# Delta-rule attention with a feed-forward part: the state step on 64 rows, behind the Gram run

## The chip, the cores and the metric

The kernel runs on one core of a Trainium2 chip. The metric is the device time of one execution in microseconds. A core has TensorE (PE; its weight loads are listed apart as PEld), VectorE (DVE), ScalarE (ACT), GpSimd (POOL) and SyncE (SP), which here only issues DMAs. Each engine works through its own instructions in a fixed order.

## What is computed

For each of 32 pairs of batch and head there is a 48x48 state that is updated token by token, 768 times; its readings are then the input of a feed-forward part.

```python
k_n = k / (np.linalg.norm(k, axis=-1, keepdims=True) + 1e-06)
for t in range(S):                                   # B, H, S, D = 4, 8, 768, 48
    y[:, :, t] = np.einsum('bhd,bhde->bhe', q[:, :, t], state)
    v_old = np.einsum('bhde,bhd->bhe', state, kt)
    state = state + bt[:, :, :, None] * np.einsum('bhd,bhe->bhde', kt, vt - v_old)
...
h = x @ w_in                                         # x: (3072, 384), w_in: (384, 2048)
return (np.maximum(0.01 * h, h) @ w_out).astype(np.float32)
```

## The kernel before

The 768 tokens are cut into 12 blocks of 64. Inside a block the recurrence is replaced by matrix products with the inverse of a triangular 64x64 matrix for each pair; the state is carried from block to block. The 32 pairs are two groups, g = 0 and 1, of 16; a group's data lies on partitions 64 to 127 (g = 0) or 0 to 63 (g = 1) of its tiles (DATA), and the state on the other half (STATE). Four streams are woven together by the loop at the end of the kernel, which runs over the blocks n and, inside a block, over 17 slots s:

- `ffn(n)` (`ff`): the feed-forward part of block n, one of 16 slices f of the hidden width in each slot. The first products go to `ph` (L735; a pair of slices is issued together, 18 matmuls), ScalarE writes `gh` and again `ph` (L745, L749), VectorE the low half `gl` (L750), and the second products add into `po` (L726), two slices later, six matmuls a slice.
- `solve(n + 1)` (`sv`): the steps of the next block, one in each of the slots that `SV` gives. `load` brings the parts of the inverse (`sq`, `rt`) and runs `pz`, `tie` runs `pu`, `kt` runs `pk` (L624) and scales the values (L640), `step_w` runs `pw` (L649), `step_y` runs `py` (L669), whose result is `ys`, and `step_s` runs `pc` (L659), the new state.
- `gram(n + 3)` (`gg`), in slot 12 in the steady blocks: `pg` (L311) holds keys times keys and keys times queries. ScalarE copies the first to `gs` (L315), SyncE stores them as `gd` (L319) and loads them as `L` (L349); VectorE masks the second into `rq` (L328) and copies corners to `gm` (L336).
- `inv(n + 2)` (`iv`): the elimination on VectorE (L392 `tmp`, L397 `T`), 31 steps of small instructions, begun by `sr` (L368) when `L` has landed. At its end ScalarE copies `T` (L457) and SyncE stores `td` and `tt` (L464, L465), from which `sq` and `rt` are loaded.

The Gram run of block n waits in program order until `solve(n - 2)` is done. `step_s` multiplies 128 rows: 64 of keys (in `rk`) with 64 of corrected values (in `rv`), and below them an identity (written once by `identities`) with the old state, so that TensorE adds the old state itself. The two groups follow each other, 16 matmuls each. ScalarE copies the result to the state rows of the next block's `rv` (L661). Results of TensorE other than `ph` and `po` share four PSUM banks in rotation (`ps_a`), in the order in which the program asks for them. A `with behind(x)` holds an instruction back in the order until the last instruction marked x; where nothing holds it, a scheduler sets the order of each engine.

In the first block VectorE and ScalarE also turn the weights, which come as raw pairs of words, into high and low halves (`conv`, `expand`, `final`, `cast`, `lows`; L193 writes the low halves `w`).

Of the kernel before, what the change touches and what calls it, by code (L numbers as in the profile page):

```python
# [20 lines left out]
D = 48  # L21
# [26 lines left out]
def delta_moe_kernel(ctx: ExitStack, tc, kq0, kqT, kv, qT, beta, cst, w_all, out, nblk):  # L48
# [47 lines left out]
    def of(x, n, g):  # L96
        return ring[x][(n * NGR + g) % NR[x]]
# [6 lines left out]
    def statics():  # L104
        for t in ring["t"]:
            nc.gpsimd.memset(t, 0.0)
        for x in "vq":
            for i, t in enumerate(ring[x]):
                nc.gpsimd.memset(t[SIDE[i % NGR]], 0.0)

    def identities():
        for i, t in enumerate(ring["k"]):
            r = SIDE[i % NGR]
            nc.gpsimd.tensor_copy(
                t[r].rearrange("p h u t -> p (h u) t"),
                eye[r, r.start:r.start + D].rearrange("p (o t) -> p o t", o=1).broadcast_to([R0, GH, D]))


    wi, wo = ([{}, {}] for _ in range(2))
    raws, mark = {}, {}  # L120
# [80 lines left out]
    def need(gen, fn, n):  # L201
        while (fn, n) not in done:
            next(gen)
# [74 lines left out]
    tails, held = [], []  # L278

    def gram(n):  # L280
        need(sv, solve, n - Q_BUFS // NGR)
        kqs = []
        for g in range(NGR):
            t = sb.tile([P, GS, NPAIR, 2, C], F32, tag="kq", name=f"kq{n}_{g}", bufs=KQ_BUFS)
# [272 lines left out]


    LD = 2
    NSLOT = LD + 4  # L560

    def fetch(n, g):
        with behind("kq"):
# [26 lines left out]
    def solve(n):  # L590
# [11 lines left out]

        def tie(g):
            merge_u(n, g, tv(n, g))

        def heads(rows):

            return ((c, u, slice(c * 64, c * 64 + rows)) for u in range(GU) for c in (1, 0))

        def quarters():  # L610

# [40 lines left out]
            mark["rv"] = d.ins  # L652

        def step_s(g):
            k, v, v1 = of("k", n, g), of("v", n, g), of("v", n + 1, g)
            pv = out_of("pc", g, D)
            for c, u, r in heads(D):
                with nullcontext() if n else behind("ph"):
                    nc.tensor.matmul(pv[r, u], k[:, c, u], v[:, c, u], start=True, stop=True)  # L659
            for c in range(2):  # L660
                nc.scalar.copy(v1[STATE[g], c], pv[c * 64:c * 64 + D])  # L661

        def step_y(g):

# [7 lines left out]
            if not n and not g:  # L672
                expand(0, "ys", slice(1, 2))

        stages = [(0, load), (1, tie), (LD, kt), (LD + 1, step_w), (LD + 2, step_y), (LD + 3, step_s)]
        if n in (0, nblk - 1):
            stages.remove((LD + 3, step_s))
        for s in range(NSLOT):
            for g in range(NGR):
                for at, stage in stages:  # L680
                    if at == s:
                        stage(g)
            if s == NSLOT - 1:
                done.add((solve, n))
                if 1 < n < nblk - 1:
                    for g in range(NGR):
                        fetch(n + 1, g)
                if n == 0:
                    columns(0)
                    yield  # L690
                    for g in range(NGR):
                        step_s(g)
            yield
# [93 lines left out]
    def weave_at(i, n, *streams):  # L787

        for gen, steps, a, b in streams:
            key = gen, n, a  # L790
            want = steps if i >= b - 1 else min(steps, max(0, i + 1 - a) * steps // (b - a))
            while taken.get(key, 0) < want:
                next(gen, None)
                taken[key] = taken.get(key, 0) + 1
# [10 lines left out]
    ff = chain(ffn, range(nblk))  # L805
    next(fg)
    statics()
    identities()
    for f in range(KA):
        load_w(f)  # L810
    for g in range(NGR):
# [38 lines left out]
    for n in range(nblk):  # L850

        for s in range(NF):
            at = min(n, 3)
            weave_at(s, n, (ff, NF, 0, NF))
            for fn, *args in work.pop(n * NF + s, ()):
                fn(*args)
            weave_at(s, n, (sv, (NS + (n == 0)) * (n + 1 < nblk), *SV[at]), (iv, NI * (n + 2 < nblk), *IV[at]),
                     (gg, NGR * (n < 2), *GG[min(n, 1)]), (gg, NGR * (0 < n < nblk - 3), *G4[min(n, 2)]))


# [2 lines left out]
KA = 2  # L863
IV, GG = ((9, 17), (6, 17), (2, 17), (2, 17)), ((2, 4), (1, 2))
G4 = (0, 1), (13, 14), (12, 13)
SV = (0, 10), (3, 13), (1, 11), (2, 12)
PD, FB = 2, 4


# [64 lines left out]
```

## Time and profile before

| | |
|---|---|
| time, median of 3 runs | 619.13 us (617.09 to 621.03) |
| profiled execution, its own time | 613.75 us |
| its span, first to last instruction | 612.0 us |
| mean granted clock of TensorE | 0.991 of full speed |
| TensorE busy | 570.2 us, 93% of the span |
| VectorE busy | 431.6 us, 71% |
| ScalarE busy | 329.5 us, 54% |
| GpSimd busy | 40.0 us, 7% |

A profile is of one execution. All windows and timelines count from the start of the span; a busy share is a mean over stretches with different limits, so a row of one stretch says nothing of another.

### The profile page before, as it was taken

The page shows a single profiled execution, that of the slowest core. Times are in us where ns is not written, and L with a number is a line of the kernel's source. Part 1 is how long each engine was busy: PE and PEld are TensorE (multiplying, and loading weights), DVE is VectorE, ACT ScalarE, POOL GpSimd, SP SyncE. Part 2 cuts the span into 40 slices and gives each one's busy share as a digit, 9 for nine tenths or more (in the row PEclk, how much of TensorE's full clock was granted, in tenths as well). Part 3 has the DMA queues.
Part 4 walks back from the last instruction along what each step waited for, and adds up shares of the span by engine and source line. Part 5 has one row for each costly group of instructions (what it writes and reads, how often), then busy time and mean ns, then how long its engine had stood idle before and what let it go on. Part 6 is the DMA issues. An engine that isn't in the chain of part 4 may idle for free.

```text
span 612.0 us, 22386 instructions
## 1 busy us (share of the span) xinstructions
PE 570.2 (93%) x9146; PEld 523.6 (86%) x9146; DVE 431.6 (71%) x1949; ACT 329.5 (54%) x818; POOL 40.0 (7%) x71
## 2 busy tenths in 40 slices
PE   5287989889899989999999999999999999999996
PEld 4266767678799989999999999999999999999996
DVE  3999899969749849759759749759759659331221
ACT  3377976735546446545545545555555545454332
POOL 7000000100040010010010010010010010100100
PEclk9989999999999999999999999999999999999999
DMA  5995933161381461570580580580661550500101
GB/s 128 304 278 207 313 80 74 39 132 31 93 162 33 96 133 33 109 152 14 108 159 7 113 158 5 119 152 12 116 146 29 98 95 4 109 6 4 27 0 27
DMA packets 120103, 59.69 MB, mean 98 GB/s; under 512 B 109248, under 2 KB 110336, under 8 KB 118976
## 3 DMA queue, kind: packets, MB, share of 16 engines
q1 hardware_dynamic: 116896, 52.42, 38.7%
q0 software_dynamic: 2528, 5.12, 3.3%
q8 instruction: 72, 1.18, 0.8%
q10 hardware_dynamic: 576, 0.72, 0.6%
q14 instruction: 31, 0.25, 0.2%
HBM read 46.96 MB, written 11.27 MB: 95 GB/s over the span
## 4 chain that ended last, share of the span: by engine, by line
PE 69%; DVE 18%; DMA 4%; issue 3%; ACT 2%; POOL 1%; SPq 1%; DVEq 0%; ACTq 0%; POOLq 0%
PE ph L735 27%; PE po L726 27%; DVE T L397 4%; DVE tmp L392 4%; PE pw L649 3%; PE py L669 3%; PE pc L659 2%; DVE w L193 2%; PE pg L311 2%; PE pk L624 2%; DVE rq L328 2%; DVE cg L179 1%; DMA L<-gd 1%; DMA sq<-tt 1%; PE pz L494 1%
## 5 line engine op out<-in xcount | busy, mean ns | idle before, releaser
L735 PE MATMUL ph<-xh,w 128*128 128x256 f32 x1056 | 205.6, 285 | 0.0
L726 PE MATMUL po<-w,gh 128*128 128x384 f32 x704 | 178.1, 344 | 0.0
L735 PEld LDWEIGHTS ph<-xh,w 128*128 128x128 f32 x1056 | 168.3, 188 | 4.8 <-issue 3.9
L745 ACT ACTIVATE gh<-ph 128x256 fp32r<-128x256 f32 (+1 forms) x192 | 73.5, 385 | 175.5 <-PE ph L735 112.1
L750 DVE TENSOR_TENSOR gl<-ph,gh 128x256 fp32r<-128x256 f32 x176 | 73.8, 420 | 130.0 <-ACT ph L749 127.4
L735 PE MATMUL ph<-xl,w 128*128 128x256 f32 x528 | 148.3, 283 | 1.6 <-DVE xl L128 1.6
L726 PEld LDWEIGHTS po<-w,gh 128*128 128x128 f32 x704 | 120.6, 188 | 3.7 <-issue 1.8
L726 PE MATMUL po<-w,gl 128*128 128x384 f32 x352 | 111.7, 338 | 2.3 <-DVE gl L750 2.3
L397 DVE TENSOR_TENSOR T<-T,tmp 128x60 f32<-128x60 f32 (+35 forms) x661 | 110.8, 206 | 0.7
L392 DVE TENSOR_TENSOR tmp<-T,L 128x60 f32<-128x60 f32 (+35 forms) x661 | 110.6, 206 | 0.4
L735 PEld LDWEIGHTS ph<-xl,w 128*128 128x128 f32 x528 | 99.5, 188 | 2.5 <-DVE xl L128 2.0
L726 PEld LDWEIGHTS po<-w,gl 128*128 128x128 f32 x352 | 65.3, 188 | 3.1 <-DVE gl L750 3.0
L749 ACT ACTIVATE ph<-ph 128x256 f32<-128x256 f32 x176 | 66.8, 380 | 0.0
L777 POOL DMA_DIRECT2D out<-ob x44 | 23.0, 527 | 482.1 <-ACT ob L776 481.5
L328 DVE TENSOR_TENSOR rq<-pg,csb 64x256 f32<-64x256 f32 x80 | 33.8, 422 | 5.7 <-ACT gs L315 4.1
L735 PE MATMUL ph<-x,cg 128*128 128x256 f32 x96 | 24.5, 407 | 4.3 <-DVE cg L179 2.8
L635 ACT ACTIVATE rt<-pk 48x512 f32<-48x512 f32 x44 | 26.1, 592 | 3.8 <-PE pk L624 3.0
L735 PEld LDWEIGHTS ph<-x,cg 128*128 128x128 f32 x96 | 18.9, 202 | 9.7 <-DVE cg L179 4.4
L661 ACT COPY rv<-pc 48x384 f32<-48x384 f32 x44 | 20.9, 475 | 9.7 <-PE pc L659 9.1
L651 ACT COPY rv<-pw 64x384 f32<-64x384 f32 x48 | 22.8, 475 | 5.5 <-PE pw L649 4.4
L640 DVE TENSOR_TENSOR rv<-rv,nt 64x384 f32<-64x384 f32 x44 | 22.5, 549 | 0.7
L726 PE MATMUL po<-cg,gh 128*128 128x384 f32 x64 | 22.7, 493 | 0.0
(101 smaller groups left out, 587.3 us busy)
## 6 DMA issues: line engine op xcount, KB each, us to landing
wr<-in_w_all SPq DMA_DIRECT2D x8, 1536.0 KB, 12.9
kq<-in_kqT SPq DMA_DIRECT2D x40, 192.0 KB, 4.4
rk<-in_kv SPq DMA_DIRECT2D x24, 192.0 KB, 3.8
rv<-in_kv SPq DMA_DIRECT2D x24, 192.0 KB, 4.0
rq<-in_qT SPq DMA_DIRECT2D x24, 192.0 KB, 3.4
L<-gd SPq DMA_DIRECT2D x18, 256.0 KB, 4.1
out<-ob POOLq DMA_DIRECT2D x44, 96.0 KB, 2.5
td<-T SPq DMA_DIRECT2D x40, 64.0 KB, 2.9
```

What stands on the lines that cost most here:

```text
L328: nc.vector.tensor_tensor(qa[to, c, b * NPAIR:(b + 1) * NPAIR], pv[b][r, 1], tri[r].rearrange("p (o t) -> p o t", o=1).broadcast_to([C, NP ...
L392: nc.vector.tensor_tensor(tv, t[:, :, j:j + 1].broadcast_to([P, k, w]), L[:, j, j + 1:].rearrange("p (o w) -> p o w", o=1).broadcast_to([P ...
L397: mark["steps"] = nc.vector.tensor_tensor(t, t, tv, ALU.subtract).ins
L635: nc.scalar.mul(ts[g][STATE[g], c], pv[g][c * C:c * C + D].rearrange("p (y v) t -> p y v t", y=2), -1.0)
L640: nc.vector.tensor_tensor(v[to, :, us], v[to, :, us], nt[to, g, :, us].rearrange("p h (u o) -> p h u o", o=1).broadcast_to([C, 2, NPAIR, D ...
L651: d = nc.scalar.copy(v[DATA[g], c], pv[c * C:(c + 1) * C])
L726: i = nc.tensor.matmul(po[t][:, :DO], a[:, ts_], w, start=(f == 0 and k == 0), stop=(f == NFC - 1 and k + 1 == len(ways)))
L735: i = nc.tensor.matmul(ph, w[:, cc * P:(cc + 1) * P], a, start=(k == 0), stop=(k + 1 == len(ways)))
L745: i = nc.scalar.activation(gh, ph, AF.Prelu, alpha=0.01)
L749: i = nc.scalar.activation(ph, ph, AF.Prelu, alpha=0.01)
L750: mark["gl"] = nc.vector.tensor_tensor(gl, ph, gh.bitcast(F32), ALU.subtract).ins
L777: nc.gpsimd.dma_start(out[r0:r0 + C], ob[a:a + C])
```

## The change

`step_s` no longer multiplies the identity: it takes the 64 rows of keys and values alone, and `both` gives it the two groups in turn, as `kt` has them, so that four quarters of the array are addressed. VectorE adds the old state while it takes the result out of PSUM; in block 0, where there is none, ScalarE copies as before. The identities go. `step_s` moves one step later, so that in the steady blocks it comes in slot 13, behind the Gram run of slot 12, and with it the end of `solve` and the loads of the next block's keys, values and queries that follow it. The Gram run waits for `step_y` of its block alone. `SV` now lists the slot of each step.

```diff
-    def identities():
-        for i, t in enumerate(ring["k"]):
...
     def gram(n):
-        need(sv, solve, n - Q_BUFS // NGR)
+        need(sv, "y", n - Q_BUFS // NGR)
...
-    NSLOT = LD + 4
+    NSLOT = LD + 5
...
         def step_s(g):
-            k, v, v1 = of("k", n, g), of("v", n, g), of("v", n + 1, g)
-            pv = out_of("pc", g, D)
-            for c, u, r in heads(D):
-                with nullcontext() if n else behind("ph"):
-                    nc.tensor.matmul(pv[r, u], k[:, c, u], v[:, c, u], start=True, stop=True)
-            for c in range(2):
-                nc.scalar.copy(v1[STATE[g], c], pv[c * 64:c * 64 + D])
+            if not g:
+                return
+            vs, v1 = ([of("v", m, g) for g in range(NGR)] for m in (n, n + 1))
+            with nullcontext() if n else behind("ph"):
+                pv = both("pc", D, lambda g, c, u: of("k", n, g)[DATA[g], c, u], lambda g, c, u: vs[g][DATA[g], c, u], D)
+            for g in range(NGR):
+                for c in range(2):
+                    x, to = pv[g][c * C:c * C + D], STATE[g]
+                    if not n:
+                        nc.scalar.copy(v1[g][to, c], x)
+                        continue
+                    with behind("gl"):
+                        nc.vector.tensor_tensor(v1[g][to, c], x, vs[g][to, c], ALU.add)
...
-        stages = [(0, load), (1, tie), (LD, kt), (LD + 1, step_w), (LD + 2, step_y), (LD + 3, step_s)]
+        stages = [(0, load), (1, tie), (LD, kt), (LD + 1, step_w), (LD + 2, step_y), (LD + 4, step_s)]
         if n in (0, nblk - 1):
-            stages.remove((LD + 3, step_s))
-        for s in range(NSLOT):
+            stages.remove((LD + 4, step_s))
+        slots = NSLOT - (not n)
+        for s in range(slots):
...
-            if s == NSLOT - 1:
+            if s == LD + 2:
+                done.add(("y", n))
+            if s == slots - 1:
                 done.add((solve, n))
...
-            want = steps if i >= b - 1 else min(steps, max(0, i + 1 - a) * steps // (b - a))
+            if isinstance(a, tuple):
+                want = sum(t <= i for t in a[:steps])
+            else:
+                want = steps if i >= b - 1 else min(steps, max(0, i + 1 - a) * steps // (b - a))
...
-SV = (0, 10), (3, 13), (1, 11), (2, 12)
+SV = (1, 2, 4, 5, 7, 8, 9, 9), (4, 6, 7, 9, 11, 12, 14), (2, 4, 5, 7, 9, 10, 13), (3, 5, 6, 8, 10, 11, 13)
```

The two lists of each place are of the same steady block, before and after the change; line numbers are those of each kernel. First TensorE, where `pc` stood before: behind the second products of slice 9 and ahead of the first products of slices 12 and 13.

```order
L669 MATMUL py_1_6010<-rv_85,rq_79 32x48 x32
L726 MATMUL po_0_5499<-w_1659,gh_9_5923 128x384 x2
L726 MATMUL po_0_5499<-w_1659,gl_9_5925 128x384
L726 MATMUL po_1_5500<-w_1659,gh_9_5923 128x384 x2
L726 MATMUL po_1_5500<-w_1659,gl_9_5925 128x384
L659 MATMUL pc_0_6068<-rv_84,rk_76 48x48 x16
L659 MATMUL pc_1_6087<-rv_85,rk_77 48x48 x16
L735 MATMUL ph_72<-xh_0_5440,w_1747 128x256
```

And where it stands now, from the end of the Gram run `pg` on.

```order
L303 MATMUL pg_1_1_6170<-kq_1_6128 64x128
L723 MATMUL po_0_5497<-w_1687,gh_11_6055 128x384 x2
L723 MATMUL po_0_5497<-w_1687,gl_11_6057 128x384
L723 MATMUL po_1_5498<-w_1687,gh_11_6055 128x384 x2
L723 MATMUL po_1_5498<-w_1687,gl_11_6057 128x384
L732 MATMUL ph_73<-xh_0_5438,w_1747 128x256
L732 MATMUL ph_73<-xl_0_5439,w_1747 128x256
L732 MATMUL ph_73<-xh_0_5438,w_1747 128x256
L612 MATMUL pc_0_6210<-rv_84,rk_76 48x48 x5
L612 MATMUL pc_1_6211<-rv_85,rk_77 48x48 x5
L612 MATMUL pc_0_6210<-rv_84,rk_76 48x48
L612 MATMUL pc_1_6211<-rv_85,rk_77 48x48
```

The state run went from ahead of the first products of slice 12 to six `po` and three `ph` behind the Gram run, inside the first products of slices 14 and 15, and the groups now take turns.

On VectorE, before, from the last instruction of the elimination to `gl` of slice 15:

```order
L397 TENSOR_TENSOR T_5558<-T_5558,tmp_30_0_6388 128x8
L750 TENSOR_TENSOR gl_12_6150<-ph_72,gh_12_6148 128x256
L750 TENSOR_TENSOR gl_13_6243<-ph_72,gh_13_6241 128x256
L328 TENSOR_TENSOR rq_78<-pg_0_0_6186,csb 64x256 x2
L328 TENSOR_TENSOR rq_78<-pg_0_1_6187,csb 64x256 x2
L328 TENSOR_TENSOR rq_79<-pg_1_0_6215,csb 64x256 x2
L328 TENSOR_TENSOR rq_79<-pg_1_1_6216,csb 64x256 x2
L750 TENSOR_TENSOR gl_14_6288<-ph_73,gh_14_6286 128x256
```

And after the change:

```order
L389 TENSOR_TENSOR T_5556<-T_5556,tmp_30_0_6386 128x8
L747 TENSOR_TENSOR gl_12_6104<-ph_72,gh_12_6102 128x256
L747 TENSOR_TENSOR gl_13_6197<-ph_72,gh_13_6195 128x256
L320 TENSOR_TENSOR rq_78<-pg_0_0_6140,csb 64x256 x2
L320 TENSOR_TENSOR rq_78<-pg_0_1_6141,csb 64x256 x2
L320 TENSOR_TENSOR rq_79<-pg_1_0_6169,csb 64x256 x2
L320 TENSOR_TENSOR rq_79<-pg_1_1_6170,csb 64x256 x2
L655 TENSOR_TENSOR rv_86<-pc_0_6210,rv_84 48x384 x2
L655 TENSOR_TENSOR rv_87<-pc_1_6211,rv_85 48x384 x2
L747 TENSOR_TENSOR gl_14_6286<-ph_73,gh_14_6284 128x256
```

The four adds came in between the eight masks and `gl` of slice 14; nothing else moved here. On ScalarE the four copies of `pc` are gone, and `gh` of slice 12 stands ahead of the copy `T`, where it stood behind it.

On the queue of SyncE, before, from the stores of the elimination's result to the load `L` that the next elimination waits for:

```order
L464 DMA td_6395<-T_5558 32x16x32 x2
L465 DMA tt_6396<-T_5558 1024x1x16
L464 DMA td_6395<-T_5558 32x16x32 x2
L465 DMA tt_6396<-T_5558 1024x1x16
L565 DMA rv_85<-in_kv 64x768
L527 DMA sq_1973<-td_6395 32x8x32
L524 DMA sq_1971<-tt_6396 32x8x32 x3
L319 DMA gd_6178<-gs_0_6184 32x8x32 x4
L319 DMA gd_6178<-gs_1_6214 32x8x32 x4
L524 DMA sq_1971<-tt_6396 32x8x32
L527 DMA sq_1973<-td_6395 32x8x32
L349 DMA L_6177<-gd_6178 64x1024 x2
```

And after the change, to the last of the loads `sq` from `tt`:

```order
L457 DMA tt_6394<-T_5556 1024x1x16
L525 DMA rt_82<-td_6393 32x16x32
L525 DMA rt_83<-td_6393 32x16x32
L311 DMA gd_6132<-gs_0_6138 32x8x32 x4
L516 DMA sq_1969<-tt_6394 32x8x32
L311 DMA gd_6132<-gs_1_6168 32x8x32 x4
L516 DMA sq_1969<-tt_6394 32x8x32
L557 DMA rk_76<-in_kv 64x768
L341 DMA L_6131<-gd_6132 64x1024 x2
L557 DMA rk_77<-in_kv 64x768
L516 DMA sq_1969<-tt_6394 32x8x32 x2
```

Three loads `sq` from `tt` went from ahead of `gd` to behind it, two of them behind `L`; two loads `rt` came ahead of `gd`; and the keys `rk`, which stood ahead of `td`, now surround `L`. The values `rv` are loaded later, outside the piece shown.

## Rows read from the trace of the kernel before

**Rows 1.** Windows, two stretches: start:end, length, busy us and instructions by engine, clock, DMA.

```profile
60.00:122.00 62.00, 57.97 (x819) 43.27 (x817) 58.56 (x185) 48.90 (x78) 2.21 (x4) 0.97 0.47 132
...
325.81:370.65 44.84, 44.84 (x731) 42.22 (x731) 33.15 (x172) 24.06 (x64) 2.08 (x4) 1.00 0.47 94
```

**Rows 2.** Timeline of TensorE, one steady block: start us, us, engine, line, op, tiles.

```profile
325.74 0.62 PE L726 MATMUL po<-w,gh 128*128 128x384 f32 x2
...
326.90 0.28 PE L735 MATMUL ph<-xh,w 128*128 128x256 f32 x1
327.02 0.28 PE L735 MATMUL ph<-xl,w 128*128 128x256 f32 x1
...
330.20 1.58 PE L649 MATMUL pw<-rv,rt 128*32 128x48 f32 x128
...
338.92 1.65 PE L659 MATMUL pc<-rv,rk 128*48 128x48 f32 x64
340.49 0.39 PE L735 MATMUL ph<-xh,w 128*128 128x256 f32 x1
...
344.01 1.94 PE L311 MATMUL pg<-kq 48*64 48x128 f32 x62
...
360.57 0.65 PE L494 MATMUL pz<-sq,gm 128*32 128x128 f32 x16
...
369.54 1.12 PE L624 MATMUL pk<-rt,rk 64*48 64x64 f32 x64
```

**Rows 3.** Groups by line and form, whole span: busy us, mean ns, idle before.

```profile
L745 ACT ACTIVATE gh<-ph 128x256 fp32r<-128x256 f32 x176 | 67.7, 385 | 172.4 <-PE ph L735 109.0 <-DVE gl L750 62.0
...
L640 DVE TENSOR_TENSOR rv<-rv,nt 64x384 f32<-64x384 f32 x44 | 22.5, 549 | 0.7
```

**Rows 4.** Timeline of VectorE, same block, with its idle time before a row.

```profile
342.06 0.17 DVE L397 TENSOR_TENSOR T<-T,tmp 128x8 f32<-128x8 f32 x1
...
345.23 0.42 DVE L750 TENSOR_TENSOR gl<-ph,gh 128x256 fp32r<-128x256 f32 x1 [0.73 <-ACT ph L749]
345.69 3.50 DVE L328 TENSOR_TENSOR rq<-pg,csb 64x256 f32<-64x256 f32 x8
350.16 0.42 DVE L750 TENSOR_TENSOR gl<-ph,gh 128x256 fp32r<-128x256 f32 x1 [0.96 <-ACT ph L749]
...
362.45 0.19 DVE L368 TENSOR_SCALAR sr<-L 128x32 uint32<-128x32 uint32 x1 [1.76 <-DMA L<-gd]
```

**Rows 5.** Timeline of ScalarE, end of the next elimination.

```profile
387.48 1.08 ACT L457 COPY T<-T 128x512 f32<-128x512 f32 x1 [0.80 <-DVE T L397]
```

**Rows 6.** Timeline of SyncE's queue, same block.

```profile
347.77 1.38 SPq L527 DMA_DIRECT2D sq<-td  x1
350.24 1.30 SPq L524 DMA_DIRECT2D sq<-tt  x3
351.63 4.14 SPq L319 DMA_DIRECT2D gd<-gs  x8
355.82 0.47 SPq L524 DMA_DIRECT2D sq<-tt  x1
...
357.25 1.13 SPq L349 DMA_DIRECT2D L<-gd  x2
```

**Rows 7.** DMA issues of the page: count, KB each, median us to landing.

```profile
sq<-tt SPq DMA_DIRECT2D x40, 32.0 KB, 2.0
```

**Rows 8.** TensorE's waits, 122 to 160 and 160 to 227 us: total, times, longest.

```profile
PE po L726 <- DVE gl L750: 2.3, 2, 1.3
...
PE pc L659 <- issue: 2.0, 1, 2.0
PE pz L494 <- DMA sq<-tt: 1.5, 1, 1.5
```

**Rows 9.** Chain that ended last, first block: start us, us, what.

```profile
112.27 0.24 DVE tmp L392 x2
...
121.61 3.42 DVE w L193 x2
```

More of the change, by code (lines that the diff above doesn't have):

```diff
@@ L109, in statics @@
                 nc.gpsimd.memset(t[SIDE[i % NGR]], 0.0)
-    def identities():
-        for i, t in enumerate(ring["k"]):
[L113 to L116, printed above, removed]
     wi, wo = ([{}, {}] for _ in range(2))
@@ L604, in tie @@
             merge_u(n, g, tv(n, g))
-        def heads(rows):
-            return ((c, u, slice(c * 64, c * 64 + rows)) for u in range(GU) for c in (1, 0))
         def quarters():
@@ L807, in delta_moe_kernel @@
     statics()
-    identities()
     for f in range(KA):
@@ L856, in delta_moe_kernel @@
                 fn(*args)
-            weave_at(s, n, (sv, (NS + (n == 0)) * (n + 1 < nblk), *SV[at]), (iv, NI * (n + 2 < nblk), *IV[at]),
+            weave_at(s, n, (sv, (NS + (n == 0)) * (n + 1 < nblk), SV[at], None), (iv, NI * (n + 2 < nblk), *IV[at]),
                      (gg, NGR * (n < 2), *GG[min(n, 1)]), (gg, NGR * (0 < n < nblk - 3), *G4[min(n, 2)]))
```

## The prediction

> **What bounds the kernel now.** I began with the windows, which give each engine's busy time by stretch. In a block of the steady part TensorE is busy 44.84 of 44.84 us and VectorE 33.15 [rows 1]; the reader is to see that TensorE has no gap there, so a microsecond less of its work can be a microsecond less of time. From 60 to 122 us it is otherwise: VectorE is busy 58.56 of 62 us [rows 1], and the chain that ended last runs through it, in the elimination (tmp and T) and in the low halves of the weights (w) [rows 9].
>
> Then the timeline of one steady block. On TensorE pc, the run that the change rewrites, holds the engine from 338.92 to the ph behind it at 340.49, which is 1.57 us, and the Gram run pg comes later, from 344.01 for 1.94 us [rows 2]. On VectorE the elimination of the next inverse ends at 342.06 + 0.17 = 342.23 us, gl of f = 13 stands at 345.23, and the eight masks (rq from pg) take 345.69 to 349.19 [rows 4].
>
> Last the queue of SyncE, since it closes a second loop that the windows don't show. The end of the elimination releases td and tt; behind them in the same queue stand the copies gd of the Gram blocks and the load L, and L starts the next elimination (sr) at 362.45 [rows 4, 6]. From 342.23 to 362.45 are 20.2 us, and from there to the next end of the elimination, at which the copy T of ScalarE starts (387.48), 25.0 us [rows 5]. So this loop takes 45.25 us against TensorE's 44.84: the two are level, and one that is shortened alone gives little.
>
> **The change part by part.** *TensorE's state run.* It has 64 records a block before and after (32 fp32 matmuls, two records each), but with 64 rows in place of 128 and both groups in turn, four quarters of the array are used where two were. No row shows 64 rows by 48 columns with 48 moving, so I bound it. pc took 1.65 us for 64 records; pk, the same quarters with 64 moving columns, 1.12 us for 64; pw, four column strips with 48 moving columns, 1.58 us for 128, which is 0.79 us for 64 [rows 2]. The new run costs between 0.79 and 1.12 us and saves 0.53 to 0.86; below pw's rate nothing in the trace lies. I take pw's rate, since pw and pc share the 48 moving columns: 0.8 us saved.
>
> The Trainium skill (TensorEngine Tiling (Array Packing), Instruction Overhead) says that a matmul has an overhead of about 60 cycles, so that one moving column takes as long as 60, and warns not to tile further where a dimension is already small. By that rule 48 moving columns would cost no less than pk's 64 nearly do, and the saving would be the 0.53 us end. The trace speaks against it: per record pw took 12.3 ns and pk 17.5 ns [rows 2], a ratio of 0.70 where the columns stand as 0.75.
>
> *VectorE's adds.* Four adds of 48x384 from PSUM and SBUF take the place of four copies on ScalarE, for every block from the second on. The nearest rows are the masks, a tensor_tensor from PSUM with 256 columns, 3.50 / 8 = 0.44 us [rows 4], and one with 384 columns from SBUF, 0.55 us [rows 3]: 1.75 to 2.2 us a block, and I take 2.1, by the like columns. In the steady part they stand behind the masks and ahead of gl of f = 14, where VectorE waited 0.96 us for ScalarE [rows 4] and has 11 us to spare in the block [rows 1]; cover there is good. In the first block there is none: VectorE is full and on the chain, and TensorE waited for gl right behind it, 2.3 us [rows 8, 9]. The 2.1 us are paid there in full, once.
>
> *Where pc now stands.* It is queued on TensorE behind pg, six po and three ph. With pc gone ahead of it, pg begins 1.57 us earlier, at 342.44, and ends at 344.38; six po (325.74 to 326.90) are 1.16 us and three ph at 0.12 are 0.36 [rows 2], so pc is reached at 345.9. It takes the PSUM banks of the first group's pg, so it now waits until the masks and the copies of that group are through, and all of ph and po is queued behind it. With the masks where they are, the first bank would be free two masks in, at 345.69 + 0.88 = 346.57, the second at 347.44: 1.5 us of wait, more than the run saves. But the masks come earlier: gh of f = 12 now stands ahead of the copy T on ScalarE, so gl of f = 12 follows the elimination at once, and after T's 1.08 us [rows 5], gh and ph of f = 13 at 0.39 each [rows 3] and one gl of 0.42 the masks start at about 342.23 + 2.28 = 344.5. That frees the banks at 345.4 and 346.3; the first is no wait, the second about 0.4 us, and none if the elimination ends half a microsecond earlier.
>
> *SyncE's queue.* Ahead of gd three loads sq from tt go away, which with their wait filled 349.15 to 351.63, 2.48 us [rows 6]; one more rt comes in, about one issue, 0.5. Between gd and L there is one issue more. L thus moves 1.4 us nearer to the elimination's end, by bounds 1.9 nearer to 0.5 farther (if the loads ahead of it wait as before). The loop is then 45.25 - 1.4 = 43.85 us, just under the 44.84 - 0.8 = 44.04 us of TensorE. The last sq, which pz needs, comes behind L and rk, about 1.5 us later than before; it was issued at 355.82 and pz ran at 360.57 [rows 2, 6], so 4.75 us less a landing of 2.0 [rows 7] were to spare; with sq 1.5 later and TensorE 0.8 earlier, half a microsecond is left.
>
> *The sum.* Seven state runs (of blocks 4 to 10) lie in the steady part; of the 0.8 us each I leave 0.2 for the bank wait and the level loop: 7 x 0.6 = 4.2 us gained. In the first block +2.1. In the stretch to 227 us the state run of block 2 saves 0.8; that of block 3 lies beside the elimination and saves nothing; and of pz's wait of 1.5 us for sq [rows 8] I take 0.9 as gone, since the Gram run there comes before the state run. Together 2.1 - 0.8 - 0.9 - 4.2 = -3.8 us. The removed GpSimd copies of the identity lie in the opening, beside loads, and count nothing; the state run of block 0 keeps its place beside VectorE's work on the weights, also nothing (uncovered, each would give under 1 us). The profiled execution, 613.75 us (span 612.0), would become 609.95; the median of the runs shown is 5.4 us above it, and 619.13 - 3.8 = 615.3 us.
>
> **The rivals.** *Everything is gained.* The elimination falls ahead of TensorE, no bank is waited for, seven runs give 0.86 each (6.0), block 2 its 0.86, and the stretch without work in the middle of its pc, 2.0 us, and pz's wait, 1.5 us [rows 8], go: 10.4 less 2.1 is 8.3, so 610.8 us. For it: VectorE has room in the steady block. Against it: the two loops are level, so one must yield as much as the other, and the 2.0 us are marked as issue, time in which the engine waits for nothing that the profile shows, and no line of the change names their cause.
>
> *The bank wait eats it.* The elimination keeps its place, pc's second bank is late by 0.4 to 0.5 us in each block, and 0.3 x 7 + 0.8 - 2.1 leaves 0.8 us: 618.3 us, no change. For it: the wait is new and stands ahead of all of ph and po. Against it: each such wait lets the elimination catch up.
>
> *The second loop becomes the bound: slower.* L stands behind two sq from tt and behind rk, and rk waits for pc. If these push L 0.5 us away from the elimination's end instead of nearer, the loop is 45.75 us, 0.9 over TensorE's period of before; pz then waits for sq in each of eight blocks, 7.2 us, with 2.1 in the first block and 0.8 saved in block 2: 627.6 us. It decides from the point at which L is later than 20 us behind the elimination's end. Against it speak the three loads that leave the queue ahead of gd. The Trainium skill (TensorEngine Tiling (Array Packing), PSUM Bottleneck) names the mechanism in general: tiling speeds up TensorE but not the emptying of PSUM, which can become the bound. Here the emptying moves to VectorE, the engine of this loop.
>
> *The change doesn't do what it says:* the listing of the order shows the new run behind pg in each block, so only its quarters could fail to overlap; pk's row shows that they do, and I give this no chance of its own.
>
> **How the numbers follow.** Forecast 0.43, everything gained 0.27, bank wait 0.20, second loop 0.10. One per cent, about what a measurement of this kernel can tell from no change, is 612.9 to 625.3 us. Faster by over 1%: the 0.27 and 0.05 of the forecast's own spread, 0.32; slower: 0.10 and 0.02 of the two middle cases, 0.12; within: 0.56. The range runs from below the first rival, 608, to 622, which leaves out most of the last; the forecast's own spread is 612 to 618.
>
> **What would show it.** Right: pc's 64 records in about 0.8 us; TensorE busy without a gap in the steady blocks, a period of 44.0 to 44.4 us between like ph; the adds at 0.5 to 0.55 us; VectorE's stretch from 102 to 125 us longer by 2.1; L to sr at 18.8 us behind the elimination's end. Wrong: a gap of TensorE ahead of pc released by a mask, a gap ahead of pz released by sq, or pc at pk's rate.

## The result: slower by 1.1%, outside the predicted range

The changed kernel takes 625.09 us, median of 9 runs (619.42 to 628.14); the kernel before, run beside it, 617.26 us, median of 9 (613.33 to 621.03). The ratio is 1.0113, 95% interval 1.0073 to 1.0154: about 7 us slower. The forecast was 615.3, the range 608 to 622. The profiled execution took 625.77 us (span 624.0). That of before, 613.75, lay near the low end of its runs, so the two profiles differ by 12 us, more than the medians do.

Below, "px 4" is the start of the transposes px with which the feed-forward of block 4 opens, and "px 4 to 11" the seven blocks from there to the same point of block 11; both are read from TensorE's timeline.

The chain that ended last, its shares by engine, in the kernel before (first line) and in the changed kernel (second):

```profile
PE 69%; DVE 18%; DMA 4%; issue 3%; ACT 2%; POOL 1%; SPq 1%; DVEq 0%; ACTq 0%; POOLq 0%
...
PE 50%; DVE 30%; DMA 6%; SPq 6%; ACT 4%; issue 4%; ACTq 0%; DVEq 0%
```

TensorE's share of the chain is 50% against 69% before; VectorE has 30% against 18%, and transfers with SyncE's queue 12% against 5%. A second loop has become the bound. The windows of two neighbouring steady blocks of the changed kernel, in the columns of [rows 1]:

```profile
315.30:359.92 44.62, 44.62 (x731) 41.99 (x730) 35.73 (x176) 21.84 (x61) 2.06 (x4) 1.00 0.45 93
359.92:406.56 46.64, 44.72 (x731) 42.05 (x730) 35.88 (x177) 21.88 (x61) 2.08 (x4) 1.00 0.44 91
```

Where TensorE has no gap, a block is 44.62 us, 0.2 less than before [rows 1]. The next block takes 46.64, and 1.92 us of it are a gap. TensorE's timeline shows where:

```profile
306.40 2.29 PE L303 MATMUL pg<-kq 48*64 48x128 f32 x62
...
310.22 1.14 PE L612 MATMUL pc<-rv,rk 64*48 64x48 f32 x64
...
371.15 0.64 PE L486 MATMUL pz<-sq,gm 128*32 128x128 f32 x16 [1.92 <-DMA sq<-tt]
```

Against [rows 2]: pc went from 1.65 us to 1.14, within 0.02 of pk's duration there, and pg grew from 1.94 to 2.29. pz waits for sq, which it did not in the block of [rows 2]. TensorE's waits, 165 to 235 us and then 235 us to the end, where the kernel before had none after 227:

```profile
PE pz L486 <- DMA sq<-td: 3.3, 1, 3.3
...
PE pz L486 <- DMA sq<-tt: 4.7, 3, 2.1
PE pz L486 <- DMA sq<-td: 1.1, 2, 0.6
```

SyncE's queue in that block, behind the end of the elimination at 351.06:

```profile
356.77 2.88 SPq L311 DMA_DIRECT2D gd<-gs  x4
359.74 0.39 SPq L516 DMA_DIRECT2D sq<-tt  x1
360.18 1.93 SPq L311 DMA_DIRECT2D gd<-gs  x4
362.16 0.45 SPq L516 DMA_DIRECT2D sq<-tt  x1
362.70 0.52 SPq L557 DMA_DIRECT2D rk<-in_kv  x1
363.74 1.13 SPq L341 DMA_DIRECT2D L<-gd  x2
...
365.55 1.18 SPq L516 DMA_DIRECT2D sq<-tt  x2
```

Three of the four sq stood ahead of gd before [rows 6]; now the four are strung out between gd, rk and L, and the last two come behind L. The chain that ended last runs through just this piece:

```profile
356.74 0.55 DVE rv L655
...
365.55 5.20 DMA sq<-tt
...
371.15 0.64 PE pz L486 x16
```

Of the last pair of sq, the one issued at 365.55 lands 5.20 us later, and the one issued at 366.19 after 4.76 us; the median before was 2.0 [rows 7]. VectorE's timeline then shows who pays for it:

```profile
350.89 0.17 DVE L389 TENSOR_TENSOR T<-T,tmp 128x8 f32<-128x8 f32 x1
...
353.18 3.53 DVE L320 TENSOR_TENSOR rq<-pg,csb 64x256 f32<-64x256 f32 x8
356.74 2.26 DVE L655 TENSOR_TENSOR rv<-pc,rv 48x384 f32<-48x384 f32 x4
...
369.35 0.19 DVE L360 TENSOR_SCALAR sr<-L 128x32 uint32<-128x32 uint32 x1
...
374.91 0.42 DVE L747 TENSOR_TENSOR gl<-ph,gh 128x256 fp32r<-128x256 f32 x1 [2.63 <-ACT ph L746]
```

The masks start 2.1 us behind the elimination's end (forecast 2.28), and sr 18.3 us behind it (20.2 before [rows 4], forecast 18.8). But the next elimination stops again at 374.91: it stands behind a gl whose ph is queued behind pz on TensorE. So the loop is: elimination, td and tt, sq, pz, ph, gl, elimination. ScalarE's timeline, in the kernel before (first two lines) and in the changed one, shows what made pg longer:

```profile
342.27 1.10 ACT L457 COPY T<-T 128x512 f32<-128x512 f32 x1 [0.43 <-DVE T L397]
...
344.23 0.19 ACT L582 COPY nt<-pn 128x32 f32<-128x32 f32 x1 [0.18 <-PE pn L575]
...
306.45 1.06 ACT L449 COPY T<-T 128x512 f32<-128x512 f32 x1 [0.42 <-DVE T L389]
307.33 0.21 ACT L574 COPY nt<-pn 128x32 f32<-128x32 f32 x1
```

nt empties the PSUM bank of pn, a small run just ahead of pg, and pg's last part takes that bank. Before, pn came when T's copy was over, and nt followed it at once. Now the Gram run has moved ahead, and nt has to wait for T's copy.

### The profile page after: what moved, and what is told of

It reads as the page before. It is cut to its first block, busy times and chain, and to the rows that moved or that the text cites. A ratio compares the mean times of both kernels' runs of the same rounds, so it can differ in the third digit from the quotient of the medians.

```text
span 624.0 us, 22352 instructions
## 1 busy us (share of the span) xinstructions
PE 571.7 (92%) x9146; PEld 524.0 (84%) x9146; DVE 452.8 (73%) x1989; ACT 307.9 (49%) x778; POOL 38.3 (6%) x69
## 4 chain that ended last, share of the span: by engine, by line
PE 50%; DVE 30%; DMA 6%; SPq 6%; ACT 4%; issue 4%; ACTq 0%; DVEq 0%
PE ph L732 21%; PE po L723 19%; DVE T L389 8%; DVE tmp L384 8%; DMA sq<-tt 2%; DVE gl L747 2%; DVE rq L320 2%; DVE w L185 2%; PE pw L637 2%; SPq L311 2%; PE py L663 2%; DMA sq<-td 2%; DVE rv L628 1%; SPq L516 1%; DVE cg L171 1%
## 5 line engine op out<-in xcount | busy, mean ns | idle before, releaser
L732 PE MATMUL ph<-xh,w 128*128 128x256 f32 x1056 | 208.4, 287 | 0.0
L732 PEld LDWEIGHTS ph<-xh,w 128*128 128x128 f32 x1056 | 170.9, 191 | 4.3 <-issue 3.4
L732 PE MATMUL ph<-x,cg 128*128 128x256 f32 x96 | 26.3, 431 | 4.0 <-DVE cg L171 3.7
L303 PE MATMUL pg<-kq 48*64 48x128 f32 x640 | 23.2, 275 | 1.4 <-issue 1.4
```

What stands on the lines that cost most here:

```text
L303: nc.tensor.matmul(ps[b][c * 64:(c + 1) * 64, p * 128:(p + 1) * 128], kq[r, c ^ b, p, 0], kq[r, c ^ b, p].rearrange("p x t -> p (x t)"), s ...
L732: i = nc.tensor.matmul(ph, w[:, cc * P:(cc + 1) * P], a, start=(k == 0), stop=(k + 1 == len(ways)))
```

## The experiments

Two theories. Q: the place of the new run puts the sq loads behind gd, rk and L on SyncE, and pz, with it the next elimination, waits for them. V: the adds load VectorE, whose elimination everything else waits for. All kernels were timed beside the kernel before; ratios are to it, with 95% intervals.

| kernel | ratio | px 4, us | px 4 to 11, us | pz waits after 235 us |
|---|---|---|---|---|
| before (profile shown above) | 1 | 261.32 | 308.55 | none |
| changed | 1.0113 (1.0073 to 1.0154) | 269.87 | 312.40 | 5.8 |
| e1 new form, old place | 1.0302 (1.0247 to 1.0357) | 277.24 | 317.47 | 9.7 |
| e2 old form, new place | 1.0082 (1.0044 to 1.0119) | 264.76 | 313.64 | 3.8 |
| e3 changed, no add | 1.0067 (1.0029 to 1.0104) | 262.43 | 316.97 | 8.6 |
| e4 changed, sq on GpSimd | 1.0090 (1.0058 to 1.0121) | 276.99 | 306.63 | 1.9 |
| e5 the same from block 5 on | 1.0005 (0.9981 to 1.0029) | 268.61 | 306.78 | none |
| e6 changed, old form in blocks 1 to 4 | 1.0050 (1.0021 to 1.0079) | 270.11 | 315.91 | 5.7 by sq |
| e7 e5 and e6 together | 0.9974 (0.9939 to 1.0009) | 263.25 | 306.29 | none |
| e8 e7, nt on VectorE | 0.9940 (0.9910 to 0.9969) | 267.56 | 306.15 | none |
| e9 before, sq on GpSimd from block 5 on | 0.9982 (0.9955 to 1.0009) | 263.98 | 310.43 | none |
| e10 changed, L on GpSimd from block 5 on | 1.0025 (0.9996 to 1.0053) | 268.41 | 311.76 | 5.0 |
| e11 e5 with the old form in all blocks | 0.9997 (0.9972 to 1.0023) | 263.00 | 309.55 | none |
| e12 e5, adds of blocks 1 to 4 twice | 1.0064 (1.0035 to 1.0092) | 271.24 | 307.41 | none |

A ratio rests on 6 to 12 runs of the kernel; px 4, px 4 to 11 and the waits are from one profiled execution each, which for e4, e6, e8 and e10 was the slowest of its kernel.

**The two parts of the change apart: e1, e2 and e3.** e1 is the kernel before with the new step_s and no identities:

```diff
-            for c in range(2):
-                nc.scalar.copy(v1[STATE[g], c], pv[c * 64:c * 64 + D])
+                        nc.vector.tensor_tensor(v1[g][to, c], x, vs[g][to, c], ALU.add)
...
```

> The kernel before with the new form of the state step alone (64 rows, the two groups in turn, the old state added by VectorE) at its old place ahead of the Gram run; SV and NSLOT as before. If the order on SyncE's queue is the cause (theory Q: with the state step behind the Gram run, two of the four loads sq from tt stand behind L and rk, pz waits for them, and the elimination waits for gl behind pz): most of the loss is gone, ratio to the kernel before 0.995 to 1.005, waits of pz for sq after 235 us under 2 us where the changed kernel has 5.8. If the adds on VectorE are the cause (theory V: 2.26 us of adds a block in an engine that is level with TensorE): as slow as the changed kernel, ratio 1.008 to 1.015, a steady period of 45.5 us or more.

e2 is the changed kernel with the old step_s (and its identities) at the new place:

```diff
-                pv = both("pc", D, lambda g, c, u: of("k", n, g)[DATA[g], c, u], lambda g, c, u: vs[g][DATA[g], c, u], D)
+            pv = out_of("pc", g, D)
+            for c, u, r in heads(D):
...
```

> The changed kernel with the old form of the state step (128 rows with the identity, one group after the other, four copies on ScalarE) at the new place behind the Gram run. Theory Q: as slow as the changed kernel or slower by pc's half microsecond a block, ratio 1.008 to 1.018, since three of the four loads sq from tt stand behind both rk and L. Theory V: no add, so the kernel before's time, ratio 0.997 to 1.003.

e3 is the changed kernel with ScalarE's copies in place of the adds. It leaves the old state out of the sum.

```diff
-                        nc.vector.tensor_tensor(v1[g][to, c], x, vs[g][to, c], ALU.add)
+                    nc.scalar.copy(v1[g][to, c], x)
```

> The changed kernel without the add: ScalarE copies pc and the old state is left out of the next one, so that four copies of about 0.47 us on ScalarE stand in place of four adds of 0.56 us on VectorE; the order of SyncE's queue stays. Theory Q: ratio 1.004 to 1.012, pz still waits 4 us or more for sq after 235 us. Theory V: ratio 0.985 to 1.000. The adds of the first block alone would account for 2 us, 0.3%, under either.

e1 met neither theory's numbers: its ratio is over both ranges, and pz waits 9.7 us where Q had under 2. At the old place the adds fall inside the elimination (at 360.15, between its last tmp at 360.07 and its last T at 362.46), and e1 loses 3%: the form needs the new place. At the new place the form hardly decides: with the old form (e2) or without adds (e3) the kernel stays 0.7% to 0.8% slower than before, and only 0.3% to 0.5% under the changed kernel, with intervals that overlap its own. Both reach px 4 within 3.5 us of before and lose their time later, most of it in pz's waits. TensorE's waits of e3 after 235 us:

```profile
PE pz L486 <- DMA sq<-tt: 7.3, 4, 2.4
```

So V isn't the cause in the steady blocks.

**The queue: e4, e5, e9 and e10.** e4 issues the loads sq from tt by GpSimd in all blocks:

```diff
-                nc.sync.dma_start(A[r, :, r], Tt[k * GU:(k + 1) * GU].rearrange("u i m -> i u m"))
+                nc.gpsimd.dma_start(A[r, :, r], Tt[k * GU:(k + 1) * GU].rearrange("u i m -> i u m"))
```

> The changed kernel with the four loads sq from tt issued by GpSimd's queue, so that they stand behind neither L nor rk. Theory Q: pz's waits for sq after 235 us fall from 5.8 to under 1 us, the steady period from 45.7 to 44.3 to 44.8 us, 5 to 9 us less than the changed kernel, ratio to the kernel before 0.995 to 1.004. Theory V: the changed kernel's time within 2 us, ratio 1.008 to 1.015.

The steady part became 306.63 us, better than before's 308.55, but the ratio of 1.0090 missed Q's 0.995 to 1.004, and pz still waited 1.9 us. px 4 came at 276.99, 7 us later than in the changed kernel. e5 below, which differs only in that the early blocks keep SyncE, is 0.85% of 618, 5.3 us, faster: in the early blocks the edit costs more than it gives. GpSimd also carries gram(4)'s transfers there; that these are what collides was not tried. e5 leaves those blocks alone:

```diff
-                nc.sync.dma_start(A[r, :, r], Tt[k * GU:(k + 1) * GU].rearrange("u i m -> i u m"))
+                (nc.gpsimd if n > 4 else nc.sync).dma_start(A[r, :, r], Tt[k * GU:(k + 1) * GU].rearrange("u i m -> i u m"))
```

> The changed kernel, with one edit: from block 5 on the four loads of the inverse's sixteen-row diagonal tiles (sq<-tt in merge_z) are issued by GpSimd instead of SyncE, so that they no longer stand behind the next block's two L loads and the key loads. Blocks 2 to 4, where GpSimd also carries gram(4)'s transfers, keep SyncE. Theory Q (the steady loss is the SyncE queue: elimination, td and tt, then sq late, then pz, ph, gl and the next elimination): after 235 us pz waits under 1 us in all instead of 5.8, a block takes 44.65 us instead of 45.7, and the six blocks from px 5 to px 11 together 262 instead of 267; the time is about 5 us under the changed kernel's, 620. The early blocks stay as in the changed kernel (px 4 at 270). Theory V (the adds on VectorE are the whole loss): the adds are unchanged, so 624 to 626, with 45.7 a block.

All of Q's numbers came: no wait of pz, 44.65 us a block, a ratio of 1.0005. With four small loads a block on another queue 1.08% of 618, 6.7 us, is back. In e5 the sq loads of a block whose elimination ends just before 394.11 go out at 400.38 on GpSimd's queue, the last at 403.04:

```profile
400.38 1.79 POOL L516 DMA_DIRECT2D sq<-tt  x3 [36.72 <-DMA tt<-T]
403.04 0.67 POOL L516 DMA_DIRECT2D sq<-tt  x1 [0.87 <-issue]
```

That is done 9.6 us behind the elimination's end, where the changed kernel needed 15.7 (351.06 to 366.73). VectorE in e5 no longer stops behind sr, and the next elimination ends 25.05 us behind it (394.11), as in the kernel before:

```profile
369.06 0.19 DVE L360 TENSOR_SCALAR sr<-L 128x32 uint32<-128x32 uint32 x1 [1.75 <-DMA L<-gd]
...
371.91 0.36 DVE L747 TENSOR_TENSOR gl<-ph,gh 128x256 fp32r<-128x256 f32 x1
```

e9 is the control: the kernel before with the same edit as e5.

> The kernel before, with the sq loads issued by GpSimd from block 5 on and nothing else: what that queue edit is worth without the change. Theory Q says nothing is won, since pz waited for no sq load after 227 us there: 44.85 a block and a ratio of 0.998 to 1.002. If the edit is worth something of its own (SyncE's queue held other work back in the kernel before as well), 0.99 to 0.995, and then the recovery of the changed kernel by the same edit says less about the change. Its first 230 us are those of the kernel before, so they show how far px 4 (261.32 in the profile of before) and the granted clock around 46 to 58 us differ between two profiles of one program: under 2 us if the difference of 8.6 us to the changed kernel is the change's.

It is no faster beyond its interval (at most 0.45%), and its steady part is not shorter (310.43 against 308.55). Most of what the edit gives back in e5 is therefore something that the change broke. e10 moves the neighbour instead:

```diff
-                    i = queue.dma_start(Lh[b0][r * 64:(r + 1) * 64].rearrange("l j i -> l (j i)"), gd.rearrange("l j i -> l (j i)"))
+                    i = (nc.gpsimd if n > 4 else queue).dma_start(Lh[b0][r * 64:(r + 1) * 64].rearrange("l j i -> l (j i)"), gd.rearrange("l j i -> l (j i)"))
```

> The changed kernel, with the two L loads of the Gram tiles from block 5 on issued by GpSimd instead of SyncE, and the sq loads left on SyncE. It tells which neighbour in SyncE's queue makes the sq loads late. If it is L, which waits for the Gram tiles to land and holds the sq loads behind it (sq issued at 365.55 behind L at 363.74 in the changed kernel): pz waits under 1.5 us after 235 us and the time is 619 to 621, as with the sq loads moved. If it is the sheer number of issues and transfers (gd, key loads, sq) in that stretch: pz still waits 3 us or more and the time is 623 to 626.

This one is mixed. The time, 618.86, fits the first case, the waits of the profile fit the second. SyncE's queue of e10 shows sq still strung out behind gd and rk, and the last line, the pair issued behind rk at 409.79, how long its loads took to land:

```profile
404.78 3.21 SPq L311 DMA_DIRECT2D gd<-gs  x4
408.04 0.45 SPq L516 DMA_DIRECT2D sq<-tt  x1
408.58 1.15 SPq L557 DMA_DIRECT2D rk<-in_kv  x2
...
sq<-tt SPq DMA_DIRECT2D x2, 32.0 KB, 5.8
```

L goes out by GpSimd's queue at 409.91, beside that pair, and the pair lands as late as behind L in one queue. So the slow landing goes with L's transfers under way, not with the place behind L in SyncE's queue. In e5 the last sq is out at 403.71 and L follows at 407.81, and the four land in 2.7 us as a median. The profiled execution, 623.55, is the slowest of its 12 (616.6 to 623.55), so the waits of the others may be shorter. By the time, L is one of the neighbours that make sq late; gd and rk are still ahead of it, and how the loss divides among them stays open.

**The early blocks: e6, e7 and e12.** e6 keeps the old form in blocks 1 to 4:

```diff
+            if n < 5:
+                step_s_old(g)
+                return
```

> The changed kernel, with the state step of blocks 1 to 4 in the old form (identity rows, 128 rows, four ScalarE copies, no add) and that of blocks 5 to 10 in the new one; place, queues and masks as changed. Theory V for the early part (2.26 us of adds a block delay eliminations that nothing covers, and the clock with them): px 4 at 262 to 263.5 instead of 269.87, as in the two kernels without adds, and the time 5 to 7 us under the changed kernel's, 618 to 620. Theory Q: the steady blocks still take 45.5 to 46.5, pz still waits 3 to 6 us for sq after 235 us, and the time stays over that of the kernel before by 0.3% to 0.8%. If neither holds in the early part (px 4 near 270): the place or the mask of the key tiles sets it, and the time is 624 to 626.

The time fell by about 0.6% of 618, 3.9 us, against the changed kernel (intervals that barely overlap), but stayed at 621.88, over the 618 to 620 of theory V. px 4, expected at 262 to 263.5, was 270.11, a miss; but the profiled execution (629.5) is the slowest of its 12, and its px 4 and waits tell little. That the steady loss stays, as Q said, is shown by e7, which differs from e6 by the queue edit alone and is 0.76% of 618, 4.7 us, faster. e7 has this and e5's edit together:

> Both edits together: old form of the state step in blocks 1 to 4, and from block 5 on the sq loads issued by GpSimd. Theory Q and V together (two separate losses): px 4 at 262 to 263.5, 44.65 us a block from there on (306.6 to px 11 against 308.6 in the kernel before), so the last px at 569 to 571 like the kernel before's 569.87, and a ratio to it of 0.995 to 1.002, 614 to 618 where the kernel before has 617 to 618. If the two losses are one (an early delay that is carried on, or a clock that goes with the new form): this gives no more than the better of the two edits alone, 619 or over.

It gave what the sum of two separate losses should: px 4 at 263.25, a steady part of 306.29, and a ratio of 0.9974, whose interval still holds 1. Against e5 alone it gains 0.3%, which is within the intervals, so that the early loss is a second one rests on e6 and e12. e12 asks from the other side, with e5 and

```diff
+                        for i in range(2 if n < 5 else 1):
```

ahead of the add.

> The kernel with the sq loads on GpSimd from block 5 on, and in blocks 1 to 4 each of the four adds issued twice (the second writes the same sums again), so that VectorE has 2.26 us more in each of these four blocks and nothing else differs. Theory V for the early part (there the elimination on VectorE is what the rest waits for, and each us of adds is paid in full or nearly so): px 4 moves from 268.6 to 272 to 278, and the ratio to the kernel before from 1.0005 to 1.006 to 1.015. If only the first block pays, as the prediction had it: 2.3 us, 1.003 to 1.005. If the adds are covered in the early blocks and the later px 4 there comes from something else (the place, the mask, chance): 1.0005 within 0.003, and px 4 at 268 to 270.

Four blocks with 2.26 us more, 9.0 in all, made the ratio 1.0064 instead of e5's 1.0005: 0.0059 x 618 = 3.6 us, and by the two intervals anything from 1.3 to 5.9 (an estimate). px 4 moved by 2.6 us and px 5 by 3.7 (316.96 against 313.28). So about two fifths of early adds are paid, and not all of them; the time doesn't tell this from the first block alone, 2.26 us. TensorE's waits do. From 165 to 200 us, around the transposes px of block 2, e11 (old form, below) had the first of these lines, e5 the next two, e12 the last two:

```profile
PE px L707 <- DVE rq L328: 0.7, 2, 0.4
...
PE px L701 <- DVE rq L320: 1.6, 2, 1.3
PE ph L732 <- DVE xl L120: 1.4, 1, 1.4
...
PE px L702 <- DVE rq L320: 0.9, 2, 0.6
PE ph L733 <- DVE xl L120: 3.7, 1, 3.7
```

TensorE waits there for VectorE's masks (rq) and for xl, a low half that VectorE writes: 0.7 us without adds, 3.0 with them and 4.6 with twice as many, each in one execution. In the other kernels at the new place it is 3.3 to 3.5 with adds in that block (the changed kernel, e4, e10) and none to 0.7 without. So block 2 pays for adds as well.

**The sizes on TensorE: e11 and e8.** e11 is e5's edit with the old form in every block.

> The changed kernel with the old form of the state step in every block (128 rows, identity, four ScalarE copies, no add) at the new place, and the sq loads issued by GpSimd from block 5 on. Against the same with the new form from block 5 on it prices the form alone where PE is the bound: pc 1.58 to 1.65 instead of 1.05 to 1.12, so 45.2 us a block against 44.65 by the sizes of the runs, six blocks 3 us, a ratio to the kernel before of 1.000 to 1.004. If ScalarE's four copies (1.95) stand in the way there as well, 45.5 a block and over 1.004; if the size of pc is hidden, 44.65 to 44.8 and 0.997 to 0.999.

A block from px to px, with its pg and pc, in e11 (first fence) and in e7 (second):

```profile
353.33 0.82 PE L707 MATMUL px<-csb,ys 128*128 128x128 f32 x6
...
389.09 2.29 PE L311 MATMUL pg<-kq 48*64 48x128 f32 x62
392.92 1.64 PE L659 MATMUL pc<-rv,rk 128*48 128x48 f32 x64
398.50 0.71 PE L707 MATMUL px<-csb,ys 128*128 128x128 f32 x5
```

```profile
397.21 0.82 PE L725 MATMUL px<-csb,ys 128*128 128x128 f32 x6
...
432.99 2.26 PE L311 MATMUL pg<-kq 48*64 48x128 f32 x62
436.79 1.13 PE L624 MATMUL pc<-rv,rk 64*48 64x48 f32 x64
441.86 0.38 PE L725 MATMUL px<-csb,ys 128*128 128x128 f32 x2
```

45.17 and 44.65 us: the form is worth 0.52 us a block once nothing else is in the way, which is pc's own 0.51. The ratio, 0.9997, came out a hair under the expected 1.000 to 1.004. And 45.17 is 0.33 over the 44.84 of [rows 1], which is what pg has lost (2.26 to 2.29 in place of 1.94). e8 takes that back, by moving nt off ScalarE:

```diff
-            nc.scalar.copy(nt.rearrange("p g h u -> p (g h u)"), ps[:, 0:HS])
+            (nc.vector.tensor_copy if n > 4 else nc.scalar.copy)(nt.rearrange("p g h u -> p (g h u)"), ps[:, 0:HS])
```

> The kernel with both edits (old form in blocks 1 to 4, sq loads from GpSimd from block 5 on), and from block 5 on the copy nt<-pn moved from ScalarE, where it stands behind the 1.06 us copy of T, to VectorE behind the gl of chunk 12. Theory N (the Gram run is longer in the changed kernel, 62 records in 2.27 us against 1.94 before, because its last bank is pn's and waits for nt): pg falls back to about 1.9, a steady block from 44.65 to 44.3, six or seven blocks 2 us less: a ratio to the kernel before of 0.993 to 0.996. If the Gram run is long for another reason (its own gs copies, or the clock): 44.65 a block and 0.997 as without the edit. If VectorE's extra 0.2 us ahead of the masks is on a path: 44.8 or more.

```profile
356.78 0.82 PE L725 MATMUL px<-csb,ys 128*128 128x128 f32 x6
...
392.54 1.94 PE L311 MATMUL pg<-kq 48*64 48x128 f32 x62
...
396.02 1.43 PE L624 MATMUL pc<-rv,rk 64*48 64x48 f32 x64
401.39 0.82 PE L725 MATMUL px<-csb,ys 128*128 128x128 f32 x6
```

pg is back at 1.94, as theory N said, but the block takes 44.61: pc behind it grew from 1.13 to 1.43. That fits a PSUM bank that pc now reaches before the masks have let it go, though no row names what it waited for. The ratio of 0.9940 is the best of all and the only one whose interval lies under 1. It fell in theory N's range, but by luck: N wanted 44.3 us a block. The steady blocks don't explain its distance to e7 (0.14 us over seven blocks), and the two intervals overlap, so whether nt's move helps stays open. With e7's two edits and this one the kernel beats the kernel before by 0.3% to 0.9%, and the changed one by more.

## Why the prediction was wrong

*The step that failed first is SyncE's last sentence*: "so 4.75 us less a landing of 2.0 were to spare; with sq 1.5 later and TensorE 0.8 earlier, half a microsecond is left." The delay was right: the last sq was issued 14.1 us behind the elimination's end before (342.23 to 356.29, [rows 4, 6]) and 15.7 after. The landing was wrong. 2.0 us was the median of all sq loads; the last pair, issued behind L and rk, took 5.2 and 4.8. TensorE was also only 0.2 us earlier and not 0.8 (pz, without its wait, would start 18.2 us behind the elimination's end; before 18.3). The half microsecond became a wait of 1.92. Worth: the changed kernel against e5, 6.7 us. The trace of the kernel before had the price. Here are the times to landing, as medians, of the three sq at 350.24 there [rows 6], of the two sq from td that it issues behind L, from 358.43 on, and of the pair at 365.55 in the changed kernel:

```profile
sq<-tt SPq DMA_DIRECT2D x3, 32.0 KB, 2.2
...
sq<-td SPq DMA_DIRECT2D x2, 32.0 KB, 4.2
...
sq<-tt SPq DMA_DIRECT2D x2, 32.0 KB, 5.0
```

A load that was to go behind L should have had the time of a load that stood there already.

*The loop that closes through pz was not in the sum.* The prediction closed it through L, and got that term nearly right (18.3 us to sr against a forecast of 18.8; before 20.2). But from sr to the end of the elimination it kept before's 25.0. In the changed kernel the next elimination ended, and T's copy began, at 397.72: 28.4 us behind sr; in e5 it was 25.05. A wait of pz is not only TensorE's: it moves the gl on which the elimination stands, then the next td and tt, and so the next sq. The rival of the second loop, 627.6 us with a chance of 0.10, named this result and pz's wait for sq, but a wrong trigger: it wanted L pushed away, and L came nearer. Nor was it VectorE's emptying of PSUM, which that rival also named: without the adds (e3) pz waits 8.6 us.

*pc was mis-sized.* I took pw's rate, 0.79 us for 64 records. It took 1.12 to 1.14, pk's duration, so 0.5 was saved and not 0.8. The bounds held the value, the choice in them was wrong. pw and pc share the 48 moving columns, but pc's weights are pk's 64x48 and pw's 128x32, as the rows name them. The sentence that the Trainium skill (TensorEngine Tiling (Array Packing), Instruction Overhead) had against it, that a matmul of one moving column takes as long as one of 60, gave the 0.53 end, and the trace of after agrees for these tiles: 48 moving columns took as long as pk's 64. For pw's tiles it doesn't: 1.58 us for 128 records with 48 moving columns [rows 2].

*pg's third of a microsecond had no term.* I moved pg ahead of pc and followed the masks and the copies of gs, but not nt, which then has to wait for T's copy on ScalarE. It is 0.33 us a block, so of the 0.8 that I gave to each steady state run 0.52 - 0.33 = 0.2 was left: e5 gains 308.55 - 306.78 = 1.8 us over its seven blocks, where I had 4.2.

*The bank wait* was forecast as 0 to 0.4 us behind masks that start 2.28 us after the elimination. They start 2.1 after it, and in the steady blocks pc began without a wait. Its price was paid one step earlier, at pg, and in block 2 at px (1.6 us in e5, 0.7 with the old form in e11); and if e8's longer pc is such a wait, whoever mends pg gets it there, at 0.3.

*The adds* took 0.55 to 0.56 us each by the chain (from 356.74 on), 2.2 a block, the upper bound (I took 2.1). That they are free in the steady blocks was right: e5 has them all and is faster there than before. "Paid there in full, once" was not: block 2 paid too, and by e12's rate of 0.4 the four early blocks pay about 3.6 us (an estimate, 1.3 to 5.9), where I had 2.1. And the gain of 0.9 on pz's early wait did not come: between 165 and 235 us pz waited 3.3 us for sq from td.

*The account.* Forecast -3.8, measured +7.0, 10.8 apart. The queue is 6.7 of it. The steady blocks gave 1.8 in place of 4.2, 2.4 more. The rest, 1.7, lies in the early blocks: e5 as a whole is 0.3 us behind the kernel before, so with 1.8 gained later they cost 2.1, where the forecast had +2.1 - 0.8 - 0.9 = +0.4. The split between steady and early blocks rests on single profiles (e9's steady part, with before's own form and place, is 1.9 us longer than before's), so it is good to about 2 us; the 6.7 of the queue rests on the runs.

## What to carry to other kernels

When a run on one engine is moved, list for every DMA queue that its step passes which load now stands behind which, and follow the last one to the engine that waits for it and on around to the engine that released it; a spare of half a microsecond, made with a median landing time, is no spare. Take the landing time from a load that stands at the same place, if the trace has one. Two loops of equal length, TensorE's own work and a loop through transfers, must both be shortened, and the cheapest way here was a load on a queue that had room at that place (not everywhere: the same edit cost time in the early blocks). For a matmul whose price no row showed, the row with the same array tile gave it here, not the one with the same moving columns.

## What was not expected of the hardware

The same load landed 2.0 us after its issue as a median before, and in the steady blocks of the changed kernel 4.0 to 5.3 us after it behind the two loads L (256 KB each by the page of the profile). With L on another queue but issued at the same time (e10) it took 4.5 to 6.6.

The granted clock of the opening differs between executions of one program. TensorE runs at one of two levels, 1.2 GHz (0.50 in the rows) and 2.4 (1.00). From 46 to 52 us the kernel before had the first of these rows, columns as in [rows 1], and e9, the same program up to block 5, the second:

```profile
46.00:52.00 6.00, 4.35 (x197) 3.66 (x196) 5.79 (x9) 4.42 (x9) 0.00 (x0) 0.83 0.22 53
...
46.00:52.00 6.00, 2.95 (x134) 2.75 (x137) 3.71 (x6) 2.94 (x6) 0.00 (x0) 0.50 0.08 25
```

From 52 to 58 us they had 1.00 and 0.94; the changed kernel had 0.50 in both. e9's px 4 was 2.7 us later, so of the 8.6 us by which the changed kernel's px 4 differs from that of before, a part of this size can be chance. The clock suggests that not all of it is: by the medians over the runs, the mean granted clock was 0.975 to 0.982 in the six kernels with adds in blocks 1 to 4 (0.975 to 0.978 in five of them), 0.980 to 0.987 in the seven others, and 0.984 to 0.986 in the kernel before. Whether the adds lower the clock or only go with it was not tried.
